# One transpose for two heads' last keys, zero-padded V tails, PV dots in every iteration: a change to a fused attention and two-MoE kernel

## Chip, cores, metric

One core of a Trainium2 chip runs the whole program: TensorE (matmuls and transposes), VectorE, ScalarE, GpSimd (named POOL in the profile), SyncE (named SP, which issues the copies), and 16 DMA engines that carry them out. The metric is the device time of one execution in microseconds (us), the median of three runs.

## What is computed

```python
# q, k, v: (4 batches, 8 heads, 576 keys, 64); tau a scalar
scores = scale * np.matmul(q, k.transpose(0, 1, 3, 2))
thresh = np.max(scores, axis=-1, keepdims=True) - tau
scores = np.where(scores >= thresh, scores, -1e9)
attn = np.exp(scores - np.max(scores, axis=-1, keepdims=True))
attn = attn / (np.sum(attn, axis=-1, keepdims=True) + 1e-09)
o = np.matmul(attn, v)
# o becomes x: (2304, 512); then two layers of this form, w_in (512, 2048), w_out (2048, 512):
h = x @ w_in; g = h - tanh(h); x = g @ w_out        # second layer: g = h * sigmoid(h)
```

## The kernel before

The attention part fills the first 327 us, the two layers the rest; the change touches the attention part alone.

*Tiling.* The 32 heads form 16 pairs (NPAIR), each two heads of one batch. A head's 576 keys are four chunks of 128 (SM = 512 keys) and a last one of 64 (SL); its 576 queries likewise. A query tile is 128 queries of one head; the ninth tile of a pair holds the last 64 queries of both heads. Two tiles form a `Double`, and one iteration n starts one Double. Two pairs 2u and 2u+1 take nine Doubles (NS = 9), so n runs over 8 units of nine iterations; n below is counted within the unit. The middle Double (n = 4) has the ninth tiles of both pairs.

*Stages of a Double.* For each of its tiles x = 0, 1: `score` (TensorE, L309: f32r products of the high and low parts of q and k into PSUM; tile `s`), `peak` (VectorE, L325: row maximum, negated), `thr1` (ScalarE, L339: threshold), `exp` (ScalarE, L329); one iteration later `keep` (VectorE, L345: zero what is under the threshold, sum up), `guard` (GpSimd, L353), `inv` (VectorE, L356), `norm` (GpSimd, L360), `flip` (TensorE, L365: four transposes of e into PSUM tile `t`); `evac` copies them to `pt` (ScalarE, L380), `flip_last` transposes the last 64 keys (L375: two transposes, which place head 0's keys in rows 0 to 63 and head 1's in rows 64 to 127) and `levac` copies them to `pj` (L392). flip0 stands at the end of the iteration after the score, flip1 and flip_last in the one after that.

*PV.* `Out` is one half (288 queries) of a pair's output: for each of five key chunks one f32 matmul ("dot") for each head, head 0 into rows 0 to 63 of PSUM tile `a`, head 1 into rows 64 to 127. The device runs every f32 dot as two passes. The last chunk's dots take 64 rows each of `pj` and of `vn` (L411, form 64*64 in the profile). `AVS` gives how many dots an iteration runs: 6 and 4 in turn, from n = 6 on, none at n = 5. `store` copies `a` to `ao` (L419) and, with the second half, to xT by DMA (L424 to L427), and then loads V of the pair after next.

*Preparing a pair.* `PREP` gives the iteration, relative to its unit, of each step for the even and the odd pair: t (four transposes of the loaded K or Q, tile `nat`, L229), f (copy back), left (transposes of the last keys and queries, L234), h (high parts, VectorE L261, with the DMA moves kh and qp, L249), l (low parts, GpSimd L274, with the moves of kl and qp; it then issues the load of the next pair's K or Q, L216). `nat` has one buffer for K and one for Q.

*Order.* The first layer's weights are decoded along the way (`DECS`: six stages of three chains, L118 to L148). `ORDER` is the order in which an iteration issues its actions. TensorE, VectorE, ScalarE and GpSimd execute their instructions in that order; the copies on SyncE's queue are placed by a planner, by when they can run, and execute one after the other, each waiting for its own conditions with all later ones behind it.

## Time and profile before

| | |
|---|---|
| median of three runs | 1106.5 us (1105.49 to 1106.54) |
| the profiled execution | 1106.72 us |
| its span, first to last instruction | 1104.9 us |
| TensorE, share of the span busy | 98% |
| VectorE, ScalarE, GpSimd busy | 72%, 71%, 34% |
| attention part | to 327 us; a unit of nine iterations takes 38.1 us |
| DMA engines busy in the attention part | about 77% |

The times of the rows below are us from the start of the span. A timeline row has its start, its length (from the first start to the last end of equal instructions that follow each other), engine, line, operation, tile written <- tiles read, shape, count, and in brackets the idle time of the engine before it and what ended that. A matmul's recorded length (0.27 to 0.45 us) is longer than the step to the next one, since matmuls are pipelined; steps are therefore read from start to start.

### The profile page before, as it was taken

Reading aid. Unit: us, or ns where it says so; the run is one execution under the profiler, and the core shown is the slowest. Engines: PE = TensorE matmul, PEld = TensorE weight load, DVE = VectorE, ACT = ScalarE, POOL = GpSimd, SP = SyncE. Lnnn points to the kernel's source line nnn. Section 1 sums busy time; section 2 is a strip of 40 time slices with the busy share of each in tenths; the row PEclk is TensorE's granted clock in tenths of the full one; section 3 lists DMA queues with packets and bytes.
Section 4 is the critical chain, followed back from the end, with each engine's and each line's share of the span. In section 5 each row is a group of like instructions: output and inputs, shape, how many; then the busy total and the mean of one; then the engine's idle time right before and its main releaser. Section 6 shows DMA issues by size and latency. Waiting matters only on the chain.

```text
span 1104.9 us, 17846 instructions
## 1 busy us (share of the span) xinstructions
PE 1086.0 (98%) x6028; PEld 903.2 (82%) x6028; DVE 799.1 (72%) x1492; ACT 780.6 (71%) x1628; POOL 370.7 (34%) x414
## 2 busy tenths in 40 slices
PE   8999999999999999999999999999999999999998
PEld 6677767777768888888889988888989899889986
DVE  5888888888857876666665678877768665775553
ACT  5999989999879887777777888855545443454342
POOL 4666766776632435334432233322100000000000
PEclk8999999999999999999999999999999999999999
DMA  8578777877633313223321011244323221232111
GB/s 207 129 189 222 194 185 196 220 194 187 167 114 149 96 43 139 107 94 133 116 76 39 1 39 58 67 148 155 122 58 95 82 65 50 63 115 68 50 32 57
DMA packets 104298, 124.93 MB, mean 113 GB/s; under 512 B 47760, under 2 KB 71824, under 8 KB 103184
## 3 DMA queue, kind: packets, MB, share of 16 engines
q1 hardware_dynamic: 104208, 123.80, 39.0%
q8 instruction: 48, 0.79, 0.3%
q14 instruction: 42, 0.34, 0.1%
HBM read 73.93 MB, written 17.30 MB: 83 GB/s over the span
## 4 chain that ended last, share of the span: by engine, by line
PE 94%; DVE 2%; DMA 1%; issue 1%; ACT 1%; SPq 0%; POOL 0%; DVEq 0%; POOLq 0%; ACTq 0%
PE bank L943 18%; PE bank L626 18%; PE bank L679 17%; PE bank L1038 16%; PE s L309 8%; PE a L411 8%; PE t L365 6%; PE t L375 2%; PE t L229 1%; DVE e L345 1%; DVE kh L261 1%; DMA nat<-in_k_dram 0%; SPq L216 0%; POOL e L360 0%; PE t L234 0%
## 5 line engine op out<-in xcount | busy, mean ns | idle before, releaser
L679 PE MATMUL bank<-g_r,wo 128*128 128x512 f32 (+1 forms) x960 | 211.0, 368 | 0.2 <-DVE g_r L665 0.2
L626 PE MATMUL bank<-xs_r,wr 128*128 128x512 f32 (+1 forms) x640 | 193.3, 368 | 0.0
L679 PEld LDWEIGHTS bank<-g_r,wo 128*128 128x128 f32 x960 | 168.4, 189 | 30.0 <-DVE g_r L665 0.4
L1038 PE MATMUL bank<-wr 128*128 128x384 f32 x816 | 189.2, 337 | 1.4 <-DVE tm_r L980 1.4
L645 POOL TENSOR_TENSOR tm_r<-tm_r 128x512 f32<-128x512 f32 (+1 forms) x78 | 96.6, 1238 | 233.1 <-ACT tm_r L640 227.6
L1038 PEld LDWEIGHTS bank<-wr 128*128 128x128 f32 x816 | 146.5, 188 | 7.1 <-DVE tm_r L980 2.2
L360 POOL TENSOR_SCALAR e<-e,den 128x576 f32<-128x576 f32 x144 | 113.8, 802 | 61.1 <-DVE den L356 51.2
L626 PEld LDWEIGHTS bank<-xs_r,wr 128*128 128x128 f32 x640 | 117.2, 189 | 20.5 <-issue 0.4
L325 DVE TENSOR_REDUCE c<-s 128x1 f32<-128x576 f32 x144 | 108.3, 753 | 33.3 <-PE s L309 30.5
L345 DVE SCALAR_TENSOR_TENSOR e<-s,c,e 128x576 f32<-128x576 f32 x144 | 115.4, 813 | 13.5 <-ACT e L329 13.5
L626 PE MATMUL bank<-xT,wr 128*128 128x512 f32 (+1 forms) x320 | 117.8, 368 | 0.0
L980 DVE TENSOR_TENSOR tm_r<-bank,tm_r 128x384 f32<-128x384 f32 x120 | 66.5, 554 | 67.9 <-PE bank L1038 66.6
L1000 ACT ACTIVATE tm_r<-tm_r 128x384 f32<-128x384 f32 x72 | 37.8, 525 | 107.0 <-DVE tm_r L980 106.7
L943 PE MATMUL bank<-wo,g_r 128*128 128x512 f32 x432 | 109.8, 392 | 0.0
L943 PE MATMUL bank<-wo,xs_r 128*128 128x512 f32 x432 | 108.8, 392 | 0.0
L329 ACT ACTIVATE e<-s,c 128x576 f32<-128x576 f32 x144 | 105.4, 732 | 0.2
L647 DVE TENSOR_TENSOR tm_r<-bank,tm_r 128x512 f32<-128x512 f32 (+1 forms) x80 | 51.0, 637 | 68.7 <-ACT tm_r L646 68.5
L943 PEld LDWEIGHTS bank<-wo,g_r 128*128 128x128 f32 x432 | 80.5, 188 | 14.7
L943 PEld LDWEIGHTS bank<-wo,xs_r 128*128 128x128 f32 x432 | 80.5, 188 | 14.4
L365 PE MATMUL t<-ident,e 128*128 128x128 f32 x576 | 83.3, 281 | 4.0 <-POOL e L360 3.1
L365 PEld LDWEIGHTS t<-ident,e 128*128 128x128 f32 x576 | 62.0, 141 | 30.7 <-POOL e L360 22.9
L657 DVE COPY_PREDICATED tm_r<-tm_r 128x512 f32<-128x512 uint32 (+1 forms) x80 | 69.6, 870 | 6.8
(126 smaller groups left out, 2008.0 us busy)
## 6 DMA issues: line engine op xcount, KB each, us to landing
wr<-pair SPq DMA_DIRECT2D x72, 256.0 KB, 3.2
st_r<-in_moe_w_out_dram SPq DMA_DIRECT2D x24, 512.0 KB, 3.6
kh<-kh SPq DMA_DIRECT2D x60, 144.0 KB, 2.6
raw<-in_moe_w_in_dram SPq DMA_DIRECT2D x16, 512.0 KB, 5.6
st_r<-in_moe_w_in_dram SPq DMA_DIRECT2D x16, 512.0 KB, 3.6
pair<-st_r SPq DMA_DIRECT2D x8, 1024.0 KB, 3.9
qp<-qh SPq DMA_DIRECT2D x30, 160.0 KB, 3.7
qp<-ql SPq DMA_DIRECT2D x30, 160.0 KB, 3.3
```

Of the source, the lines that this page charges most:

```text
L309: nc.tensor.matmul(out=s[:, j, 0:HALF], lhsT=l, rhs=r(slice(j * HALF, (j + 1) * HALF)), start=(x == 0), stop=(x == len(mms) - 1))
L325: nc.vector.tensor_reduce(out=self.c[:, x:x + 1], in_=self.s[x], axis=AX.XY, op=ALU.max, negate=True)
L329: nc.scalar.activation(out=e.rearrange("p (a b) -> p a b", a=2), in_=self.s[x], func=ACTF.Exp, bias=self.c[:, x:x + 1], scale=1.0)
L345: nc.vector.scalar_tensor_tensor(out=e2, in0=self.s[x], scalar=self.c[:, 2 + x:3 + x], in1=e2, op0=ALU.is_ge, op1=ALU.mult, accum_out=self ...
L360: nc.gpsimd.tensor_scalar(out=e, in0=e, scalar1=self.den[:, 2 + x:3 + x], scalar2=1.0, op0=ALU.mult, op1=ALU.mult)
L365: nc.tensor.transpose(t[:, c, :], self.e[x][:, c * P:(c + 1) * P], ident)
L411: nc.tensor.matmul(out=self.a[r], lhsT=lhs, rhs=rhs, start=(c == 0), stop=(c == NC))
L626: nc.tensor.matmul(out=h, lhsT=wi[:, a, cs], rhs=b, start=(c == 0 and x == 0), stop=(c == KD - 1 and x == 2))
L645: (nc.vector if u[0] == 0 and u[1] in PM else nc.gpsimd).tensor_tensor(out=r, in0=r, in1=uu, op=ALU.mult)
L679: nc.tensor.matmul(out=o, lhsT=wo[:, a, cs], rhs=b, start=(m == 0 and x == 0), stop=(m == KF - 1 and x == 2))
L943: nc.tensor.matmul(out=o, lhsT=l[:, cs], rhs=r, start=(g == 0 and low and x == 0), stop=(g == NG - 1 and not low and x == 2))
L1038: nc.tensor.matmul(out=acc, lhsT=w[:, at(a, c):at(a, c) + P], rhs=b[:, c], start=(k not in (2, 5, 6) and c == 0 and x == 0), stop=(c == 1 ...
```

## The change

- K of head 1 is loaded in another order of keys: the last 64 keys first, then the 512 others. For pairs 1 to 15 a K load has five copies for two. `e` of both tiles is one buffer of 2 x 576 columns, so head 0's last 64 keys and head 1's last 64 keys lie side by side, and one transpose of 128 columns takes the place of two. The flips of head 1 start at column 64. In the ninth tile (n = 4), whose rows belong to both heads, head 1's score products are written back into the common order, with three matmuls (288, 224 and 64 columns) for two.
- V's last keys lie in `vz`, one tile for each parity of pair, 128 rows per head, of which the other head's 64 rows are zero. The last chunk's dots have 128 rows. Two copies for one.
- `AVS` gives 5, 5, 6, 4, 5, 5, 4, 5 and 1 dots in iterations 6, 7, 8, 0, 1, 2, 3, 4, 5.
- One threshold instruction for both tiles (`thr`), after exp 0.
- Each half output is stored by its own DMA (`AOH`); V's load is an action of its own (`v`), an iteration after the store.
- `PREP`: the odd pair's K transposes and copy back one iteration earlier. `DECS` and `ORDER` anew.

```diff
-PREP = ({'tk': -6, 'fk': -5, 'left': -4, 'hk': -4, 'lk': -4, 'tq': -4, 'fq': -3, 'hq': -3, 'lq': -3},
-        {'tk': -1, 'fk': 0, 'left': 0, 'hk': 0, 'lk': 0, 'tq': 0, 'fq': 1, 'hq': 1, 'lq': 1})
-DECS = ((-4, -3, -2, -1, -1, -1), (0, 1, 2, 3, 3, 4), (2, 3, 4, 4, 6, 7))
-AVS = (6, 4, 6, 4, 6, 4, 6, 4)
-AVX = (0, 0, 0, 0, 0, 0, 0, 0)
-
-ORDER = (0, 10, 'flip1', 'f', 'evac0', 'store', 'evac1', 'keep0', 'score0', 'last', 'levac', 'keep1', 'guard', 3, 12, 'dx', 'score1', 'peak0', 'thr0', 'exp0', 'inv', 'norm0', 'norm1', 2, 13, 'peak1', 'thr1', 'exp1', 1, 11, 'dy', 't', 'warm', 'flip0', 4, 14, 'h', 5, 15, 'moves', 'l')
+PREP = ({'tk': -6, 'fk': -5, 'left': -4, 'hk': -4, 'lk': -4, 'tq': -4, 'fq': -3, 'hq': -3, 'lq': -3}, {'tk': -2, 'fk': -1, 'left': 0, 'hk': 0, 'lk': 0, 'tq': 0, 'fq': 1, 'hq': 1, 'lq': 1})
+DECS = ((-4, -2, -2, -1, -1, 0), (0, 2, 3, 4, 4, 4), (-1, 3, 3, 4, 7, 7))
+AOH = 1
+AVS = (((6, 5), (7, 5)), ((8, 6), (9, 4)), ((10, 5), (11, 5)), ((12, 4), (13, 5), (14, 1)))
+
+ORDER = (2, 'f', 'flip1', 'v', 11, 'keep0', 'score0', 'keep1', 3, 'store', 'evac0', 'evac1', 5, 1, 'guard', 'last', 10, 'peak0', 'inv', 0, 'norm0', 'levac', 13, 14, 'score1', 'norm1', 'peak1', 12, 4, 'dots', 'warm', 'exp0', 'h', 'thr', 'exp1', 'moves', 15, 'l', 't', 'flip0')
...
+                src = a[b, h0:h0 + 2, 0:SM, :].rearrange("h (p c) d -> p c h d", c=NC)
+                last = a[b, h0:h0 + 2, SM:S, :].rearrange("h p d -> p h d")
+                if x or p == 0:
+                    parts = [(t[:, 0:NC].rearrange("p c h d -> p (c h) d"), src), (t[0:SL, NC, :, :], last)]
+                else:
+                    parts = [(t[:, 0:NC, 0, :], src[:, :, 0]), (t[SL:P, 0:NC, 1, :], src[0:SL, :, 1]),
+                             (t[0:SL, 1:NC + 1, 1, :], src[SL:P, :, 1]), (t[0:SL, NC, 0, :], last[:, 0]), (t[0:SL, 0, 1, :], last[:, 1])]
                 return [lambda o=o, i=i: nc.sync.dma_start(out=o, in_=i) for o, i in parts]
...
+                vn = vns[p] = vn_p.tile([P, 2 * NC, D], F32, tag="vn", name="vn")
                 nc.sync.dma_start(out=vn[:, 0:2 * NC, :].rearrange("p (h c) d -> p h (c d)", h=2),
                                   in_=v[b, h0:h0 + 2, 0:SM, :].rearrange("h (p c) d -> p h (c d)", c=NC))
-                nc.sync.dma_start(out=vn[:, 2 * NC, :], in_=v[b, h0:h0 + 2, SM:S, :])
+                for h in range(2):
+                    nc.sync.dma_start(out=vz[p % 2][h * SL:(h + 1) * SL, h, :], in_=v[b, h0 + h, SM:S, :])
...
+                    mms = [(qh[:, cs], kl[x], x) for x in heads] + [(qp[:, x, cs], kp[:, x], x) for x in heads]
+                for i, (l, r, x) in enumerate(mms):
                     for j in range(2):
-                        nc.tensor.matmul(out=s[:, j, 0:HALF], lhsT=l, rhs=r(slice(j * HALF, (j + 1) * HALF)),
-                                         start=(x == 0), stop=(x == len(mms) - 1))
+                        if x == 0 or t < NS - 1:
+                            cuts = [(0, HALF, j * HALF)]
+                        else:
+                            cuts = ([(0, HALF, SL)], [(0, SM - HALF, SL + HALF), (SM - HALF, HALF, 0)])[j]
+                        for y, z, f in cuts:
+                            nc.tensor.matmul(out=s[:, j, y:z], lhsT=l, rhs=r[:, f:f + z - y], start=(i == 0),
+                                             stop=(i == len(mms) - 1), skip_group_check=len(heads) > 1)
...
+                        both = sm_p.tile([P, 8], F32, tag="c", name="c")
+                        self.c, self.den = both[:, 0:4], both[:, 4:8]
...
-                    e = self.e[x] = e_p.tile([P, S], F32, tag="e", name="e")
+                    if x == 0:
+                        self.both = e_p.tile([P, 2 * S], F32, tag="e", name="e")
+                    e = self.e[x] = self.both[:, x * S:(x + 1) * S]
...
+                def thr(self):
+                    nc.scalar.activation(out=self.c[:, 2:4], in_=self.c[:, 0:2], func=ACTF.Identity, bias=neg_tau, scale=-1.0)
...
+                    at = SL if x and self.tiles[x][0] and self.tiles[x][1] < NS - 1 else 0
                     for c in range(NC):
-                        nc.tensor.transpose(t[:, c, :], self.e[x][:, c * P:(c + 1) * P], ident)
+                        nc.tensor.transpose(t[:, c, :], self.e[x][:, at + c * P:at + (c + 1) * P], ident)
...
                 def flip_last(self):
-
                     t = self.tj = ps_t.tile([P, 4 * P], F32, tag="t", name="t")
...
+                    if self.tiles[0][1] == NS - 1:
+                        cuts = [(x, x, h) for x in range(2) for h in (1, 0)]
+                    elif self.tiles[0][0] == 0:
+                        cuts = [(0, h, h) for h in (1, 0)]
+                    else:
+                        nc.tensor.transpose(t[:, 0:P], self.both[:, SM:SM + P], ident)
+                        return
+                    for at, x, h in cuts:
+                        nc.tensor.transpose(t[0:(h + 1) * SL, at * P:(at + 1) * P], self.e[x][:, SM - h * SL:S], ident)
...
-                        lhs, rhs = (vn[:, h * NC + c, :], pt[:, h, c, js]) if c < NC else (vn[r, 2 * NC, :], pj[r, js])
+                        lhs, rhs = (vn[:, h * NC + c, :], pt[:, h, c, js]) if c < NC else (vz[self.p % 2][:, h, :], pj[:, js])
...
+                    if AOH:
+                        b, hp = divmod(self.p, HP)
+                        ao = ao_p.tile([P, HALF], F32, tag=f"ao{self.j}", name="ao")
+                        nc.scalar.copy(out=ao, in_=self.a)
+                        dst, at = xF[:, hp, b * S:(b + 1) * S], self.j * HALF
+                        cuts = [(at, at + HALF)]
+                        if b % 2 and self.j:
+                            cuts = [(at, SM), (SM, S)]
+                        for x, y in cuts:
+                            to = x if b % 2 == 0 else (x + SL if x < SM else x - SM)
+                            nc.sync.dma_start(out=dst[:, to:to + y - x], in_=ao[:, x - at:y - at])
+                        return
...
+            for z in vz:
+                for h in range(2):
+                    nc.gpsimd.memset(z[(1 - h) * SL:(2 - h) * SL, h, :], 0.0)
...
-            for go in (k1l, q1l, k1, q1):
+            for go in (*lk1[3:], q1l, *lk1[0:3], q1):
...
                             if o.j == 1 and o.p + 2 < NPAIR:
-                                load_v(o.p + 2)
+                                vloads.append(o.p + 2)
+
+                    def vload():
+                        while vloads:
+                            load_v(vloads.pop(0))
```

## Rows read from the trace of the kernel before

**Rows 1.** Page, part 4: the chain of waits, shares by engine
```profile
PE 94%; DVE 2%; DMA 1%; issue 1%; ACT 1%; SPq 0%; POOL 0%; DVEq 0%; POOLq 0%; ACTq 0%
```

**Rows 2.** Windows, five periods of 38.1 us: busy us by engine, mean last
```profile
sum 190.50, PE 187.33 PEld 136.64 DVE 163.29 ACT 175.04 POOL 132.71; mean PE 37.47 PEld 27.33 DVE 32.66 ACT 35.01 POOL 26.54
```

**Rows 3.** Timeline of TensorE's matmuls: start us, length, work, [idle before]
```profile
228.16 0.60 PE L229 MATMUL t<-ident,nat 128*128 128x128 f32 x4
228.94 1.38 PE L365 MATMUL t<-ident,e 128*128 128x128 f32 x8 [0.19 <-POOL e L360]
230.70 0.53 PE L309 MATMUL s<-kl,qh 128*128 128x288 f32 x2 [0.39 <-DVE e L345]
...
234.00 1.09 PE L365 MATMUL t<-ident,e 128*128 128x128 f32 x8
234.92 0.50 PE L309 MATMUL s<-kl,qh 128*128 128x288 f32 x2
...
235.53 0.38 PE L375 MATMUL t<-ident,e 128*128 128x128 f32 x2
235.74 0.51 PE L309 MATMUL s<-xT,qh 128*128 128x288 f32 x2
...
236.44 0.71 PE L411 MATMUL a<-pt,vn 128*64 128x288 f32 x4
...
237.71 1.22 PE L365 MATMUL t<-ident,e 128*128 128x128 f32 x8
...
240.34 1.68 PE L411 MATMUL a<-pt,vn 128*64 128x288 f32 x12
241.95 0.66 PE L229 MATMUL t<-ident,nat 128*128 128x128 f32 x4
242.44 1.04 PE L365 MATMUL t<-ident,e 128*128 128x128 f32 x8
```

**Rows 4.** Timeline of SyncE's queue, the even pair's moves and K load
```profile
229.94 2.44 SPq L249 DMA_DIRECT2D kh<-kh  x4
232.79 0.47 SPq L249 DMA_DIRECT2D xT<-kl  x1
233.38 1.46 SPq L216 DMA_DIRECT2D nat<-in_k_dram  x2
234.93 1.20 SPq L249 DMA_DIRECT2D qp<-qh  x2
```

**Rows 5.** Timeline of TensorE, the last output's dots
```profile
323.96 2.16 PE L411 MATMUL s<-pt,vn 128*64 128x288 f32 x16
326.06 0.70 PE L411 MATMUL s<-pj,vn 64*64 64x288 f32 x4
```

**Rows 6.** Lines of ScalarE, 55 to 284 us: threshold; busy us, mean ns
```profile
L339 ACT ACTIVATE c<-c,cols 128x1 f32<-128x1 f32 x108 | 32.1, 297 | 13.5 <-DVE c L325 11.7
```

**Rows 7.** Timeline of VectorE: kh's cast in n=5; peak 1 and keep 0
```profile
229.03 0.89 DVE L261 CAST kh<-nat 128x576 fp32r<-128x576 f32 x1
...
240.76 0.73 DVE L325 TENSOR_REDUCE c<-s 128x1 f32<-128x576 f32 x1
241.76 0.82 DVE L345 SCALAR_TENSOR_TENSOR e<-s,c,e 128x576 f32<-128x576 f32 x1 [0.27 <-ACT e L329]
```

**Rows 8.** DMA issues, 55 to 284 us: count, KB, median us to landing
```profile
nat<-in_k_dram SPq DMA_DIRECT2D x12, 32.0 KB, 3.3
```

**Rows 9.** Tile nat, 55 to 284 us: K and Q loads, issue to landing
```profile
DMA to landing us min/median/max: 2.8/3.6/5.0
```

**Rows 10.** Timeline of SyncE's queue: the odd pair's last qp moves
```profile
217.81 1.18 SPq L249 DMA_DIRECT2D qp<-ql  x2
```

**Rows 11.** Timeline of TensorE: that pair's first use of qp
```profile
223.59 0.69 PE L309 MATMUL s<-kh,qp 128*128 128x288 f32 x4
```

**Rows 12.** Timeline of TensorE at the start: pair 1's K transposes
```profile
10.88 1.07 PE L229 MATMUL t<-ident,nat 128*128 128x128 f32 x4 [2.43 <-DMA nat<-in_k_dram]
```

**Rows 13.** Waits of weight loads, 55 to 284 us: total, times, longest
```profile
PEld t L365 <- POOL e L360: 14.0, 39, 0.4
```

More of the change, by code (lines that the diff above doesn't have):

```diff
@@ L180 @@
             pk_p = pool("pk", 1)
-            e_p = pool("e", 4)
+            e_p = pool("e", 2)
             sm_p = pool("sm", 6)
@@ L195 @@
             khs = [pk_p.tile([P, 2, S], F32R, name=f"kh{i}") for i in range(2)]
+            vz = [pk_p.tile([P, 2, D], F32, name=f"vz{i}") for i in range(2)]
             nat, vns, qhs, pts = {}, {}, {}, {}
@@ L339, in thr1 @@
                         nc.scalar.activation(out=o, in_=i, func=ACTF.Identity, bias=neg_tau, scale=-1.0)
+                def thr(self):
+                    nc.scalar.activation(out=self.c[:, 2:4], in_=self.c[:, 0:2], func=ACTF.Identity, bias=neg_tau, scale=-1.0)
                 def keep(self, x):
-                    if x == 0:
-                        self.den = sm_p.tile([P, 4], F32, tag="den", name="den")
                     e2 = self.e[x].rearrange("p (a b) -> p a b", a=2)
@@ L363, in flip @@
                     t = self.tt[x] = ps_t.tile([P, NC, P], F32, tag="t", name="t")
+                    at = SL if x and self.tiles[x][0] and self.tiles[x][1] < NS - 1 else 0
                     for c in range(NC):
-                        nc.tensor.transpose(t[:, c, :], self.e[x][:, c * P:(c + 1) * P], ident)
+                        nc.tensor.transpose(t[:, c, :], self.e[x][:, at + c * P:at + (c + 1) * P], ident)
                 def flip_last(self):
                     t = self.tj = ps_t.tile([P, 4 * P], F32, tag="t", name="t")
-                    self.copies = []
-                    for x, (p, ti) in enumerate(self.tiles):
-                        for h in ((1, 0) if ti == NS - 1 else () if x == 0 else (1, 0)):
-                            js = x if ti == NS - 1 else 0
-                            e = self.e[x if ti == NS - 1 else h]
-                            nc.tensor.transpose(t[0:(h + 1) * SL, js * P:(js + 1) * P], e[:, SM - h * SL:S], ident)
+                    if self.tiles[0][1] == NS - 1:
[7 more added lines that the diff above has]
+                        nc.tensor.transpose(t[0:(h + 1) * SL, at * P:(at + 1) * P], self.e[x][:, SM - h * SL:S], ident)
                 def evac(self, x):
@@ L427, in store @@
                             nc.sync.dma_start(out=dst, in_=ao)
-            avs = {6 + i: (i // 4, i // 2 % 2, AVX[i], n - AVX[i]) for i, n in enumerate(AVS)}
+            assert all(sum(n for _, n in split) == 2 * NC + 2 for split in AVS)
+            avs = {i: (o // 2, o % 2, n) for o, split in enumerate(AVS) for i, n in split}
             outs, aos = {}, {}
             def av_at(n):
-                for i, (x, j, nx, ny) in avs.items():
+                for i, (x, j, k) in avs.items():
                     u, r = divmod(n - i, NS)
                     if r == 0 and 0 <= u < NPAIR // 2:
-                        return outs.setdefault((2 * u + x, j), Out(2 * u + x, j)), nx, ny
-                return None, 0, 0
+                        return outs.setdefault((2 * u + x, j), Out(2 * u + x, j)), k
+                return None, 0
             def due(table, n):
@@ L474 @@
             his, ts, dbl, later = {}, {}, {}, []
-            (k0, k0l), (q0, q0l), (k1, k1l), (q1, q1l) = load(0, 0), load(0, 1), load(1, 0), load(1, 1)
+            (k0, k0l), (q0, q0l), lk1, (q1, q1l) = load(0, 0), load(0, 1), load(1, 0), load(1, 1)
             for go in (k0, q0, k0l, q0l):
@@ L558, in moves @@
                             later.pop(0)()
-                    acts = {"last": last_keys, "levac": last_evac, "store": store, "moves": moves,
-                            "dx": lambda: dots(nx), "dy": lambda: dots(ny),
+                    acts = {"last": last_keys, "levac": last_evac, "store": store, "moves": moves, "v": vload,
+                            "dots": lambda: dots(dots_n),
                             "t": lambda: some("t", transposed), "f": lambda: some("f", filled),
@@ L573 @@
                     acts["inv"] = lambda: d1 and d1.inverse()
+                    acts["thr"] = lambda: d0 and d0.thr()
                     for what in ORDER:
```

15 lines of the change are left out of this document (4 added, 11 removed).

## Prediction

> **What bounds the kernel now.** I read the chain of waits first: TensorE holds 94% of it [rows 1]. Then the attention part by stretches of 38.1 us, since everything repeats with one "period" of nine iterations n = 0 to 8 (two pairs of heads; there are eight periods). In a period TensorE is busy for 37.47 us, ScalarE for 35.01, VectorE for 32.66, GpSimd for 26.54 [rows 2]: TensorE sets the pace, ScalarE is close behind. Then TensorE's timeline [rows 3]. It is nearly gapless; the one real hole is the iteration without PV dots, n = 5. There the flips start 0.78 us after the four K/Q transposes (228.16 to 228.94), where the same step takes 0.49 later (241.95 to 242.44), and the eight flips last 1.76 us until the scores (228.94 to 230.70) where 0.92 is enough (234.00 to 234.92): 1.1 us of waiting for GpSimd's norm and VectorE's keep. So what TensorE has to do counts almost one to one, and what engines beside it save counts little. Last I read SyncE's queue, which issues every copy, one after the other; from the kh moves on it has hardly a pause [rows 4].
>
> **The change part by part.** The terms are made against the profiled execution: 1106.72 us, of which 1104.9 are the span; the median of the runs is 1106.5, 0.2 below it.
>
> *On TensorE.* (a) One transpose for both heads' last keys: two take 0.21 us (235.53 to 235.74), one goes, in 60 iterations (15 pairs by 4): -6.3. (b) A slot of dots (one pass of each head): 12 passes take 1.61 us (240.34 to 241.95) [rows 3] and 16 take 2.10 (323.96 to 326.06) [rows 5]. Two slots cost 0.49, one 0.24. The four slots of a session that ends in the 64-row form last 1.27 (236.44 to 237.71); without a change of form they would last 1.61 - 0.49 = 1.12. The zero-padded V saves 0.15 for each of 32 outputs: -4.8. (c) Nine sessions of dots in a period, not eight; beside its slots a session has a fixed part of 1.61 - 6 x 0.24 = 0.17: +1.4 over eight periods. (d) The new sessions have 5, 5, 6, 4, 5, 5, 4, 5 and 1 dots. Dots alternate between the heads, and an odd number leaves one head's two passes alone in the array: 5 dots take 6 slots, 1 takes 2. That is 46 slots a period against 40: 6 x 0.24 x 8 = +11.5. No session of before is odd. If a lone head's two passes could share a slot the price would be 0; I take 11.5, because no two passes in the rows take less than 0.24. (e) The last query tile needs three score matmuls for two in head 1's rotated order, 30 more of 64 columns: 0 at the least, if they hide beside their weight loads, 0.105 at the most, a transpose's price as in (a). Taken 0.1: +3.0. Sum: +4.8. But the lone dot falls into n = 5, where TensorE waits for 1.1 us, and its 2 x 0.24 + 0.17 = 0.65 hides there: -5.2. If that hole closes in another way, the 5.2 are due. Net: -0.4.
>
> One rule speaks about (d). The Trainium skill, "TensorE: Matmul & The Clock Gate", section "The mechanism" on packing small matmuls, says that matmuls start and end strictly in program order. With both passes of head 0 ahead of both of head 1, 6 dots would then take 7 slots, 4 take 5 and 5 take 6; a period would go from 48 slots to 49, and (d) would be 1.9. The trace speaks against it: seven slots and nine slots of 0.24 are 1.68 and 2.16 us, and the rows have 1.61 and 2.10 with the fixed part in them [rows 3, 5].
>
> *ScalarE and the new wait.* One threshold instruction for two takes 0.3 us an iteration [rows 6] off an engine that does not end last: 0. In exchange head 0's keep waits for head 1's peak as well. Behind that keep stand keep 1 and both peaks on VectorE, and TensorE's next scores wait for it. Peak 1 starts at 240.76 and takes 0.73; with 0.3 for the threshold keep 0 could start at 241.8, and it starts at 241.76 now [rows 7]: 0 to 0.1 an iteration, 7 in all at most, and less than nothing where the threshold now comes late on ScalarE. Taken 0, since TensorE's work per iteration is mostly longer than this loop.
>
> *SyncE's queue: the K load.* This term decides. Head 1's keys are rotated at loading, by five copies where there were two, for 15 pairs. And PREP moves the odd pair's K transposes from n = 8 to n = 7, while their load is still issued in n = 5, behind the even pair's kl. Follow one period. VectorE casts kh from 229.03 to 229.92 [rows 7]; SyncE issues four kh moves from 229.94, the kl move at 232.79 and K's load from 233.38; two issues last until the next at 234.93, so 0.73 or more each [rows 4]. Of five the last is issued at 233.38 + 4 x 0.73 = 236.3. A small K copy lands 3.3 us after its issue in the median [rows 8], all K and Q copies between 2.8 and 5.0 [rows 9]: 239.6 (239.1 to 241.3). In n = 7 the transposes stand between dots and flips, at 237.71 now; six slots for four of the old form add 0.34, the transpose saved in n = 7 takes 0.11 off: 237.9. TensorE works in order, so flips and the next scores queue behind. It stands for 1.7 us (1.2 to 3.4) in each of seven periods: +11.9. Before, these transposes came at 241.95 [rows 3], over two us after 239.6: that was the cover, and the move takes it away. The Q load behind it in the queue comes 2.2 us later too, but the stall itself gives that time back.
>
> *qp of the odd pair.* Its last move is issued at 218.4 [rows 10]; 3.3 later is 221.7, 5.0 later 223.4, and the scores want it at 223.59 [rows 11]. Three more K issues (2.2) stand ahead of it, V's two copies leave. So it is late by 0 to 1 us a period: taken 0.3 x 7 = +2.1.
>
> *Start.* TensorE waits 2.43 us for pair 1's K [rows 12]; now two more issues of 0.73 stand ahead of its last large piece: +1.5. *At nothing:* half outputs stored one by one (16 issues more, 0.7 each at most on SyncE, after the moves in n = 6), V's load as an action of its own, four small memsets beside the first loads, decode steps that change places on engines with 3 to 11 us free in a period [rows 2]; if one lands ahead of a peak or an exp it costs up to an iteration's share of that work, which the range holds.
>
> Sum: -0.4 + 11.9 + 2.1 + 1.5 = +15.1, so 1121.8, and 1122 as a median.
>
> **The rivals.** *1. The copies are in time, and waits go.* If K's pieces are issued ahead of the moves or land sooner, 11.9 and 2.1 fall away. With dots in every iteration and less on ScalarE, waits for GpSimd's norm may go as well: 14.0 us in six periods [rows 13], 2.3 a period, of which up to 1.1 is spent above. Half of the rest is 0.6 x 8 = 5: 1106.7 - 0.4 + 1.5 - 5 = 1103, 1098 if all goes. For it: the planner places copies by when they are ready. Against: all five wait for the buffer that the kl subtraction reads, and the kh moves are ready before. Chance 0.23. *2. The copies are in time and nothing else is won:* 1106.7 - 0.4 + 1.5 = 1108; 0.12. *3. SyncE falls behind altogether:* with three K, one V and up to two output issues more between the even pair's kh moves and the odd one's, the odd pair's moves slip by their 6 x 0.73 less the pauses, 1 to 2 us beyond the forecast, in each period: 1122 + 7 x 1.5 = 1132; 0.12. For it: qp's slack is under two us. Against: the stall in n = 7 gives SyncE time. *4. Matmuls in program order,* as weighed in (d): 1122 - 9.6 = 1112; 0.03.
>
> **How the numbers follow.** The forecast, 1122, has 0.50. Its bounds: 1.2 to 3.4 for the K stall (1118 to 1134), 0 for lone dots (1110), 7 for the new wait (1129). The range, 1100 to 1132, leaves out the half of rival 3 and about a third of rival 1, under 2 in 10 with the forecast's own upper edge. About 0.2% can be told from no change. Faster: rival 1 and 0.01 of rival 2, 0.24; same: 0.09 of rival 2; slower: the forecast, rivals 3 and 4 and 0.02 of rival 2, 0.67.
>
> **What the profile after would show.** K stall: once a period TensorE's K transposes wait for the load from in_k, one to three us, behind the dots. (a), (b): one transpose between the two scores, no 64-row dots. (d): 5 dots last as long as 6, 1.6 us. n = 5 without its 1.1 us. The prediction is wrong if the K load lands before the dots of n = 7 end; then the time is near 1105, and nearer 1095 if lone passes cost nothing.

## The result, and the profile after

The changed kernel takes 1114.5 us in the median (1111.4 to 1116.2), the kernel before 1106.5 on the same chip: a ratio of 1.0067, 95% interval 1.0049 to 1.0086. It is slower by 8.0 us, where 15.5 were forecast. The profiled execution has a span of 1113.8 us, 8.9 more than before.

Where the 8.9 lie, read from TensorE's timeline: the first score starts at 11.76 (11.88 before). The seven periods from there last 274.8 (269.5 before): +5.3. From the last period's start to the first matmul of the layers it is 46.6 (45.3): +1.3. The layers take 780.54 (778.25): +2.3. But the periods are no longer equal. They last 42.7, 38.9, 37.8, 40.3, 38.4, 38.8 and 38.0; before, all but the first two were 38.1. TensorE's waits, 15 to 325 us (in total, times, longest), name the reason:

```profile
PE t L234 <- DMA nat<-in_k_dram: 4.0, 3, 1.7
PE t L380 <- POOL e L374: 2.8, 7, 0.9
PE t L239 <- DMA nat<-in_q_dram: 2.6, 3, 1.3
PE s L319 <- DVE e L359: 1.6, 4, 0.5
PE t L234 <- ACT e L342: 1.2, 1, 1.2
```

L234 are the K transposes, L239 those of the last keys and queries. The line with "ACT e" is a load as well: at 166.34 the transposes start 0.09 after K's last piece has landed, when that exp had long ended. Two periods on TensorE's timeline, n = 7 and what follows (columns as in [rows 3]):

```profile
85.26 0.94 PE L428 MATMUL a<-pt,vn 128*64 128x288 f32 x5
85.80 0.41 PE L428 MATMUL a<-pj,vz 128*64 128x288 f32 x1
86.04 0.41 PE L428 MATMUL a<-pt,vn 128*64 128x288 f32 x1
86.04 0.88 PE L428 MATMUL a<-pj,vz 128*64 128x288 f32 x3
88.26 0.63 PE L234 MATMUL t<-ident,nat 128*128 128x128 f32 x4 [1.33 <-DMA nat<-in_k_dram]
...
237.89 1.67 PE L428 MATMUL a<-pt,vn 128*64 128x288 f32 x10
239.49 1.09 PE L380 MATMUL t<-ident,e 128*128 128x128 f32 x8
...
241.72 0.94 PE L428 MATMUL a<-pt,vn 128*64 128x288 f32 x5
...
243.32 0.66 PE L234 MATMUL t<-ident,nat 128*128 128x128 f32 x4
...
245.94 1.68 PE L428 MATMUL a<-pt,vn 128*64 128x288 f32 x12
247.54 1.32 PE L380 MATMUL t<-ident,e 128*128 128x128 f32 x8
```

In the first period TensorE waits 1.33 for K, and its transposes start at 88.26; in the other they follow the dots without a pause, at 243.32, 0.33 after K's last piece landed. The same rows show the slots: 10 passes last 1.60 (237.89 to 239.49), 12 last 1.60 (245.94 to 247.54). Now SyncE's queue in the same two periods, with [rows 4] to compare:

```profile
78.66 3.97 SPq L254 DMA_DIRECT2D kh<-kh  x4
82.73 0.54 SPq L254 DMA_DIRECT2D xT<-kl  x1
83.37 3.30 SPq L220 DMA_DIRECT2D nat<-in_k_dram  x5
...
235.17 2.41 SPq L254 DMA_DIRECT2D kh<-kh  x4
237.68 0.55 SPq L254 DMA_DIRECT2D xT<-kl  x1
238.32 3.25 SPq L220 DMA_DIRECT2D nat<-in_k_dram  x5
```

Five issues take 3.25 to 3.30, 0.66 each. What differs is ahead of them: four kh moves take 2.41 in one period and 3.97 in the other, since the fourth, at 80.53, lasts 2.10 where 0.6 is usual. The fifth piece was issued at 86.08 and landed at 88.12. By size of the copy, 55 to 284 us (count, KB, median us to landing; the answer to [rows 8]):

```profile
nat<-in_k_dram SPq DMA_DIRECT2D x12, 128.0 KB, 2.7
nat<-in_k_dram SPq DMA_DIRECT2D x24, 64.0 KB, 2.8
nat<-in_k_dram SPq DMA_DIRECT2D x24, 16.0 KB, 2.3
```

The two small pieces land 2.3 us after their issue in the median, the last of them mostly 2.0 to 2.3, not 3.3. TensorE stands for K in four of the seven periods. In three of these a kh move ahead of the load lasts 1.5 to 2.1 us; in the fourth the last piece lands 3.5 us after its issue (162.71 to 166.25). In the other three periods it lands 0.25 to 0.36 us ahead of TensorE.

### The profile page after: what moved, and what is told of

Read it like the earlier page. It is cut to its first block, busy times and chain, and to the rows that moved or that the text cites. A ratio compares the mean times of both kernels' runs of the same rounds, so it can differ in the third digit from the quotient of the medians.

```text
span 1113.8 us, 17983 instructions
## 1 busy us (share of the span) xinstructions
PE 1087.3 (98%) x5998; PEld 908.6 (82%) x5998; DVE 802.2 (72%) x1492; ACT 772.5 (69%) x1556; POOL 372.7 (33%) x418
## 3 DMA queue, kind: packets, MB, share of 16 engines
q1 hardware_dynamic: 107712, 123.80, 38.4%
## 5 line engine op out<-in xcount | busy, mean ns | idle before, releaser
L374 POOL TENSOR_SCALAR e<-e,c 128x576 f32<-128x576 f32 x144 | 116.4, 821 | 71.8 <-DVE c L370 61.7
L359 DVE SCALAR_TENSOR_TENSOR e<-s,c,e 128x576 f32<-128x576 f32 x144 | 111.5, 810 | 12.9 <-ACT c L355 12.9
L1038 ACT ACTIVATE tm_r<-tm_r 128x384 f32<-128x384 f32 x72 | 37.8, 525 | 106.1 <-DVE tm_r L1018 106.0
L428 PE MATMUL a<-pt,vn 128*64 128x288 f32 x496 | 80.7, 419 | 0.0
```

Of the source, the lines that this page charges most:

```text
L359: nc.vector.scalar_tensor_tensor(out=e2, in0=self.s[x], scalar=self.c[:, 2 + x:3 + x], in1=e2, op0=ALU.is_ge, op1=ALU.mult, accum_out=self ...
L374: nc.gpsimd.tensor_scalar(out=e, in0=e, scalar1=self.den[:, 2 + x:3 + x], scalar2=1.0, op0=ALU.mult, op1=ALU.mult)
L428: nc.tensor.matmul(out=self.a[r], lhsT=lhs, rhs=rhs, start=(c == 0), stop=(c == NC))
```

## The experiments

All were timed beside the kernel before on the same chip. The last column is the difference of the two medians; the median of the kernel before moves by 1.2 us between the chips.

| kernel | median us | ratio to before, 95% interval | us to before |
|---|---|---|---|
| changed kernel | 1114.5 | 1.0067 (1.0049 to 1.0086) | +8.0 |
| changed, K by two copies, unrotated | 1105.4 | 0.9989 (0.9979 to 0.9999) | -1.2 |
| changed, K transposes moved back | 1112.2 | 1.0055 (1.0033 to 1.0077) | +5.7 |
| changed, even dots | 1110.7 | 1.0036 (1.0024 to 1.0048) | +4.2 |
| changed, halves stored together | 1115.3 | 1.0080 (1.0068 to 1.0093) | +8.7 |
| changed, K rotated on ScalarE | 1110.5 | 1.0043 (1.0030 to 1.0057) | +4.1 |
| the same, even dots ("R") | 1105.5 | 0.9998 (0.9988 to 1.0007) | -0.9 |
| R, two thresholds | 1109.1 | 1.0035 (1.0022 to 1.0047) | +3.7 |
| R, last transpose twice | 1109.1 | 1.0030 (1.0019 to 1.0042) | +3.8 |
| R, one buffer for half outputs | 1106.4 | 1.0005 (0.9996 to 1.0014) | +1.0 |
| before, five copies of K | 1112.0 | 1.0057 (1.0041 to 1.0074) | +5.6 |
| before, K transposes earlier | 1103.8 | 0.9987 (0.9977 to 0.9996) | -1.6 |
| before, both | 1108.9 | 1.0027 (1.0017 to 1.0038) | +2.9 |
| before, 5 dots everywhere | 1115.1 | 1.0080 (1.0065 to 1.0094) | +8.7 |
| before, one threshold | 1106.6 | 1.0009 (1.0001 to 1.0018) | +0.6 |
| before, padded V | 1144.1 | 1.0344 (1.0330 to 1.0358) | +38.1 |
| before, padded V, one threshold, K earlier | 1137.6 | 1.0294 (1.0272 to 1.0316) | +31.6 |
| before, padded V loaded later | 1105.1 | 0.9991 (0.9982 to 1.0000) | -0.5 |
| the same, K earlier | 1104.3 | 0.9987 (0.9978 to 0.9996) | -1.3 |

The length of an iteration (from one score 0 to the next on TensorE's timeline), in a period without a wait for a load, is what most of the readings below rest on (median over such periods):

| n | 0 | 1 | 2 | 3 | 4 | 5 | 6 | 7 | 8 | sum |
|---|---|---|---|---|---|---|---|---|---|---|
| before | 4.47 | 3.96 | 3.77 | 4.42 | 4.63 | 4.37 | 4.22 | 3.90 | 4.40 | 38.1 |
| changed, K by two copies | 4.20 | 3.97 | 3.91 | 3.90 | 5.11 | 4.03 | 4.23 | 4.31 | 3.84 | 37.5 |
| changed, K rotated on ScalarE | 4.20 | 3.97 | 3.91 | 3.90 | 5.12 | 4.04 | 4.33 | 4.32 | 4.56 | 38.4 |
| R | 4.20 | 3.98 | 3.91 | 3.90 | 4.86 | 4.03 | 4.33 | 3.89 | 4.50 | 37.6 |
| R, two thresholds | 4.19 | 3.98 | 3.91 | 3.91 | 4.68 | 4.04 | 4.68 | 3.91 | 4.77 | 38.1 |
| R, last transpose twice | 4.36 | 4.00 | 3.91 | 3.91 | 4.97 | 4.37 | 4.15 | 4.09 | 4.49 | 38.2 |
| before, 5 dots everywhere | 4.93 | 3.96 | 4.05 | 4.33 | 5.09 | 4.37 | 4.22 | 4.10 | 4.33 | 39.4 |
| before, K transposes earlier | 4.46 | 3.96 | 3.76 | 4.42 | 4.63 | 4.37 | 4.22 | 4.06 | 3.95 | 37.8 |
| before, padded V loaded later | 4.32 | 3.96 | 3.77 | 4.42 | 4.56 | 4.37 | 4.22 | 3.90 | 4.40 | 37.9 |

### The copies of K

Two copies in the changed kernel, which leave out the rotation of head 1's keys, so that its keys and values do not fit together:

```diff
-                if x or p == 0:
+                if True:
                     parts = [(t[:, 0:NC].rearrange("p c h d -> p (c h) d"), src), (t[0:SL, NC, :, :], last)]
...
```

> The changed kernel with K loaded by two copies as before, in the common order of keys; head 1's rotation is left out of the load, while everything behind it works as if it were there, so head 1's keys and values do not fit together and that part of the computation is changed. The instructions on all other engines are the same. Theory (three more issues on SyncE's queue in each period make K late at n = 7 and Q's last queries late at n = 0): both stalls go, 5 and 3.5 us in the trace of the changed kernel, and with the start some 9 us: 1105.5. Rival (the stalls come from moving the K transposes, not from the number of copies; SyncE's queue is late with two as well): 0 to 3 us, 1111 to 1114.

Measured: -1.2 to the kernel before, 9.1 less than the changed kernel. Every period but the first lasts 37.5, and no wait for K or Q is left. So the five copies cost 9.1 us, and all the rest of the change together gains about 1. That 1 is what is left of two opposite parts: in the profiled executions the first matmul of the layers starts 3.4 us earlier than in the kernel before (323.28 for 326.69), and the layers take 2.95 longer (781.20 for 778.25). Of this trace, TensorE's waits to 315 us:

```profile
PE t L380 <- POOL e L374: 2.5, 6, 0.8
PE s L319 <- DVE e L359: 1.1, 3, 0.4
```

The K transposes moved back in the changed kernel (the odd pair's part of `PREP`):

```diff
-... {'tk': -2, 'fk': -1, 'left': 0, ...
+... {'tk': -1, 'fk': 0, 'left': 0, ...
```

> The changed kernel with the odd pair's K transposes and copy back where they were before (n = 8 and n = 0 for n = 7 and n = 8), all else as changed. Theory (the K load with five copies lands after the dots of n = 7): in the trace of the changed kernel n = 7 lasts 5.37, 5.68, 4.32, 5.57, 5.25, 4.21 us, an excess of about 5 us in all over 4.2; with the transposes an iteration later, the load has landed, so about 5 us less: 1109.5, and n = 7 of one length of some 3.8 us in all periods. Rival (the queue of copies is behind in any case and the stall moves to the next step that waits for a load, Q's last keys at n = 0): no gain, 1113 to 1116, and n = 0 or n = 8 longer by what n = 7 loses.

Measured: 2.2 less, not 5, and the two intervals overlap. The stall at n = 7 went (4.0 to 4.1 in all periods), but n = 0 now lasts 5.1, 5.7, 4.6, 5.5, 7.6, 4.6, 4.2, where 4.2 is its length with two copies. The last columns wait for Q, the load behind K in the queue (in the longest of these, the scores ahead of them also stand 0.8 us for the kl and qp moves); TensorE's timeline of this kernel:

```profile
166.04 0.28 PE L239 MATMUL t<-ident,nat 64*128 64x64 f32 x1
167.33 0.27 PE L239 MATMUL t<-ident,nat 64*128 64x64 f32 x1 [1.02 <-DMA nat<-in_q_dram]
```

That is the rival. The changed kernel shows the same by itself: its n = 7 lasts 6.1, 5.7, 4.3, 5.6, 5.2, 4.3, 4.4 (the expectation's 5.37 for the first counts from its score 1) and the n = 0 behind each 4.2, 4.4, 5.7, 4.2, 5.2, 4.2, 4.9. Where K has stalled, Q mostly does not, and the other way round: the queue's lateness is paid about once a period, by the first step that needs a load.

In the kernel before, K by five copies in the old order of keys, the move, and both:

```diff
-                parts = [(main, a[b, h0:h0 + 2, 0:SM, :].rearrange("h (p c) d -> p c h d", c=NC)),
-                         (t[0:SL, NC, :, :], a[b, h0:h0 + 2, SM:S, :].rearrange("h p d -> p h d"))]
...
+                    parts = [(t[:, 0:NC, 0, :], src[:, :, 0]), (t[0:SL, 0:NC, 1, :], src[0:SL, :, 1]),
+                             (t[SL:P, 0:NC, 1, :], src[SL:P, :, 1]), (t[0:SL, NC, 0, :], last[:, 0]), (t[0:SL, NC, 1, :], last[:, 1])]
...
-... {'tk': -1, 'fk': 0, 'left': 0, ...
+... {'tk': -2, 'fk': -1, 'left': 0, ...
```

> The kernel before, with K of pairs 1 to 15 loaded by five copies for two, in the old order of keys; all else as before, the K transposes at n = 8. Prediction's steps: K lands over two us before its transposes, so only the start (1.5) and the odd pair's qp (2.1) cost: 1110. Theory formed from the run with the transposes moved back (the queue pays for its three issues once in a period, at the first step that needs a load, and that is then Q's last columns at n = 0): n = 0 some 1 us longer in each period, 1112 to 1115. Rival (five copies cost nothing where the transposes are not moved): 1106.5.

> The kernel before with the odd pair's K transposes and copy back one iteration earlier, as in the change, and nothing else: two copies of K. In its trace K lands at 238.0 where TensorE would come to the transposes at 237.7. Theory (the number of copies is what costs, the move by itself little): 0 to 0.3 us a period, 1106.5 to 1108.5. Rival (the cover of over two us that the move takes away is the price, as the prediction has it): 1 us a period or more, 1113 and up.

> The kernel before with K in five copies and the odd pair's K transposes one iteration earlier, both together, in the old order of keys: the two edits that the prediction's main term is made of, alone. Prediction's step (the fifth piece lands 1.7 us after TensorE comes to the transposes, in each of seven periods; qp and the start on top): 1106.5 + 15.5 = 1122. Theory after the runs so far (the queue's lateness is paid once a period, less its slack, wherever the first step stands that waits): as with five copies and no move, 1110 to 1114.

Five copies in the old order of work cost 5.6, more than the 3.6 of the prediction's steps, though K lands in time: in four of seven periods n = 4, where qp of the odd pair is first used, is up to 1.1 longer, and n = 0 or n = 3 in others. In one of the four TensorE stands 0.57 us ahead of scores that read qp (108.72), in another 0.44 ahead of those that read kl (186.08). The move alone gains 1.6 (n = 8 falls from 4.40 to 3.95, n = 7 grows from 3.90 to 4.06). Both together cost 2.9, which is 4.4 more than the move alone, and not 15.5. There n = 7 has no stall, 4.05 to 4.17 in all seven periods; what is late is again n = 3, n = 4 or n = 0. So with these two edits alone the stall that the prediction names does not occur.

The rotation without more copies, on ScalarE where the transposes are copied back:

```diff
+                if x == 0 and p:
+                    nc.scalar.copy(out=flat(p, 0)[0:D, 0:SM], in_=t[0:D])
+                    nc.scalar.copy(out=flat(p, 0)[D:P, SL:S], in_=t[D:P])
+                    return
...
```

> The changed kernel with K loaded by two copies in the common order; head 1's keys are brought into the rotated order where ScalarE copies the transposes back (two copies of half the partitions for one, at two places, for each K: about 0.9 us more on ScalarE, twice in a period). Theory (five copies on SyncE's queue are what costs): as with the unrotated load of two copies, 1105.4, plus 0 to 3 us for ScalarE where its copy holds an exp up: 1105 to 1109, and n = 7 and n = 0 of one length in all periods. Rival (ScalarE sets the iteration's length as much as TensorE, so 1.8 us a period come back in full): 1105.4 + 14 = 1119.

Measured: 3.8 less than the changed kernel, between theory and rival. The periods are equal again, 38.4, but n = 8 lasts 4.56 for 3.84 with two copies alone. Its timeline there, of ScalarE, VectorE and TensorE:

```profile
199.98 0.58 ACT L246 COPY nat<-t 64x512 f32<-64x512 f32 x1 [0.38 <-ACT e L350]
200.57 0.59 ACT L247 COPY nat<-t 64x512 f32<-64x512 f32 x1
...
204.16 0.82 DVE L367 SCALAR_TENSOR_TENSOR e<-s,c,e 128x576 f32<-128x576 f32 x1 [1.30 <-ACT c L363]
205.09 0.50 PE L327 MATMUL s<-kl,qh 128*128 128x288 f32 x2 [0.39 <-PE t L388]
```

ScalarE copies K back in two pieces of 0.6 us for one, its exps and threshold come later, VectorE's keep 0 waits 1.30 for the threshold (0.52 with two copies alone), and the next score 0 starts behind keep 0, which ends at 204.98.

### The dots

```diff
-AVS = (((6, 5), (7, 5)), ((8, 6), (9, 4)), ((10, 5), (11, 5)), ((12, 4), (13, 5), (14, 1)))
+AVS = (((6, 6), (7, 4)), ((8, 6), (9, 4)), ((10, 6), (11, 4)), ((12, 4), (13, 4), (14, 2)))
```

> The changed kernel with even numbers of dots in every iteration: 6, 4, 6, 4, 6, 4, 4, 4, 2 for 5, 5, 6, 4, 5, 5, 4, 5, 1. Theory (a dot without its partner of the other head costs a slot of its own of 0.24 us): six slots fewer in each of eight periods, 6 x 0.24 x 8 = 11.5 us less: 1103. Rival 1 (program order, any number of dots costs one slot more than half its number): 49 slots either way, no change, 1114.5. Rival 2 (slots saved in some iterations are not TensorE's to give, since VectorE and ScalarE set the length there): half or less of it, 1108 to 1112.

> The same kernel, K by two copies and rotated on ScalarE, with even numbers of dots (6, 4, 6, 4, 6, 4, 4, 4, 2). With no stall for a load in the way, this is the price of a dot without its partner by itself. Theory of the prediction (0.24 us for each of 48 slots): 11.5 us less than the kernel with odd numbers. Rival (an iteration cannot be shorter than the loop from a score over peak, reciprocal, two norms and a flip to the next score, 3.9 us, and most iterations of the changed kernel are at or near it): the 0.24 us at n = 4 alone comes back, 1 to 3 us less.

In the kernel before:

```diff
-AVS = (6, 4, 6, 4, 6, 4, 6, 4)
+AVS = (5, 5, 5, 5, 5, 5, 5, 5)
```

> The kernel before with 5 dots in each of eight iterations, for 6 and 4 in turn. Prediction's price (a dot without its partner takes a slot of 0.24 us, and TensorE is the bound): four iterations of a period get two slots more, 8 x 0.24 x 8 = 15.4: 1122. Rival 1 (two of these four iterations, n = 2 and n = 7 of 3.76 and 3.89 us, are set by the loop over VectorE and GpSimd and hide most of it; n = 0 and n = 4 pay): 7 to 10 us, 1114 to 1117. Rival 2 (program order, 5 and 5 cost as many slots as 6 and 4): 1106.5.

Measured: 3.8 less with the loads in the way, 5.0 less without (kernel R against the same with odd dots), 8.7 more for 5 dots everywhere in the kernel before. That is a third to little more than half of 0.24 a slot (11.5, 11.5, 15.4), and the table of iterations tells where the rest is lost. In the kernel before, two slots more cost 0.46 at n = 0 and n = 4, 0.28 at n = 2 and 0.20 at n = 7. In kernel R two slots less give back 0.43 at n = 7 and 0.26 at n = 4, and nothing at n = 2: 3.91 either way. Its timeline there, of TensorE, VectorE and GpSimd:

```profile
211.56 0.51 PE L327 MATMUL s<-kl,qh 128*128 128x288 f32 x2
212.38 0.76 DVE L344 TENSOR_REDUCE c<-s 128x1 f32<-128x576 f32 x1 [0.43 <-PE s L327]
213.05 0.15 DVE L378 RECIPROCAL c<-c 128x2 f32<-128x2 f32 x1
213.37 1.63 POOL L382 TENSOR_SCALAR e<-e,c 128x576 f32<-128x576 f32 x2 [0.47 <-DVE c L378]
...
214.17 0.66 PE L388 MATMUL t<-ident,e 128*128 128x128 f32 x4
215.06 0.66 PE L388 MATMUL t<-ident,e 128*128 128x128 f32 x4 [0.23 <-POOL e L382]
215.47 0.51 PE L327 MATMUL s<-kl,qh 128*128 128x288 f32 x2
```

Score 0 at 211.56, its peak at 212.38, behind it on VectorE the reciprocal at 213.05, the two norms from 213.37 to 215.00, flip 1 at 215.06, the next score 0 at 215.47: 3.91 round. TensorE waits 0.23 for the norm. With five dots it does not wait, and the iteration lasts as long. This loop closes in every iteration and is a floor under it; TensorE's work counts only where it is longer.

### The other parts

The transpose that the change saves, issued twice in R, and two thresholds in R:

```diff
+                        nc.tensor.transpose(t[:, P:2 * P], self.both[:, SM:SM + P], ident)
                         nc.tensor.transpose(t[:, 0:P], self.both[:, SM:SM + P], ident)
...
-... 'exp0', 'h', 'thr', 'exp1', ...
+... 'thr0', 'exp0', 'h', 'thr1', 'exp1', ...
```

> The same kernel of 1105.5 with the one transpose of both heads' last keys issued twice, the first into a part of the tile that nobody reads: the price of the transpose that the change saves. Prediction's step (TensorE counts almost one to one, 0.105 x 60): 6.3 us more, 1111.8. Rival (the iterations that lie on the loop over peak, reciprocal, norms and flip hide it, n = 1, 2, 3 above all): 1 to 3 us, 1106.5 to 1108.5.

> The kernel with K by two copies, rotated on ScalarE, and even dots (1105.5), with two threshold instructions as before, each ahead of its exp or behind it as it was, so that head 0's keep no longer waits for head 1's peak; ScalarE has some 0.3 us more in each iteration. Prediction's step (the merged threshold and its wait are worth nothing either way): 1105.5. Rival 1 (the new wait holds keep 0 up by up to 0.1 us in each of 72 iterations): 3 to 7 us less, 1099 to 1102. Rival 2 (ScalarE's 0.2 to 0.3 us an iteration are due where its exps stand on the loop): 3 to 10 us more, 1109 to 1115.

One more transpose in 60 iterations costs 4.7 (3.8 + 0.9); the prediction had 6.3. It is not 0.1 in each: n = 0, 4, 5 and 7 grow by 0.16, 0.11, 0.34 and 0.20, n = 6 shrinks by 0.18, and n = 1, 2, 3 and 8 stay as they were within 0.02. Two thresholds cost 4.6, where the prediction had 0; the table shows it at n = 6 (+0.35) and n = 8 (+0.27), with n = 4 shorter by 0.18. In the kernel before the merged threshold gains nothing:

```diff
-... 'peak0', 'thr0', 'exp0', 'inv', 'norm0', 'norm1', 2, 13, 'peak1', 'thr1', 'exp1', ...
+... 'peak0', 'exp0', 'inv', 'norm0', 'norm1', 2, 13, 'peak1', 'thr', 'exp1', ...
```

> The kernel before with one threshold instruction for both tiles, behind exp 0 as in the change; nothing else. Undoing this edit in the other kernel cost 0.47 us in each period. Theory (0.3 us less on ScalarE ahead of exp 0 and exp 1 counts in the iterations that lie on the loop over exp): 3 to 4 us less, 1102.5 to 1103.5. Prediction's step (nothing either way): 1106.5. Rival (head 0's keep waits for head 1's peak and threshold): up to 7 us more, 1108 to 1113.

There n = 2 grows from 3.77 to 3.96 and n = 4 from 4.63 to 4.76, which n = 3, n = 6 and n = 8 nearly give back: +0.6. So the merged threshold's worth depends on the order around it; which waits make n = 6 and n = 8 of R longer with two was not traced further.

Zero-padded V in the kernel before, its load right behind the output's store, and then one iteration later as in the change (the last two):

```diff
-                nc.sync.dma_start(out=vn[:, 2 * NC, :], in_=v[b, h0:h0 + 2, SM:S, :])
+                for h in range(2):
+                    nc.sync.dma_start(out=vz[p % 2][h * SL:(h + 1) * SL, h, :], in_=v[b, h0 + h, SM:S, :])
...
-... (vn[r, 2 * NC, :], pj[r, js])
+... (vz[self.p % 2][:, h, :], pj[:, js])
...
-                                load_v(o.p + 2)
+                                vloads.append(o.p + 2)
```

> The kernel before with V's last keys zero-padded for each head (128 rows in the last dots, no 64-row form), loaded by two copies for one; nothing else. Prediction's step: 0.15 for each of 32 outputs, 4.8 us less, 1101.7. Theory after the runs so far (of what TensorE saves, the iterations with n = 2 and n = 7, near the floor of 3.8 to 3.9 us, give back little): about half, 2 to 4 us less, 1102.5 to 1104.5. Rival (the 15 copies more on SyncE's queue take it back): 1106.5 or more.

> The kernel before with three parts of the change and without the rotated K: one threshold instruction, V's last keys zero-padded, the odd pair's K transposes one iteration earlier. Theory (these are the parts that gain, the five copies and the odd numbers of dots are those that cost): -1.5 for the move as measured, -3 to -4 for the threshold, -2 to -5 for V: 1096 to 1100. Rival (they all shorten the same iterations and do not add up): 1100 to 1103.

> The kernel before with V's last keys zero-padded, loaded by two copies for one, and V's load issued an iteration later than the output's store, as the change does it; nothing else. In the run without that delay SyncE came to V's load ahead of the odd pair's kh moves and waited there for V's buffer, and n = 4 lasted 10 us. Theory: with the load behind Q's, that wait is gone, and what is left is the saving in the last dots, 2 to 5 us: 1101.5 to 1104.5. Rival (one issue more for each pair on SyncE's queue costs as much as it saves): 1106.5. Second rival (the queue still comes to V too early): 1115 or more.

> The same with the odd pair's K transposes one iteration earlier (two copies of K, the old order of keys, the old dots). Theory: the move's gain of 1.5 and the saving in the last dots add up: 1100 to 1103, less than both kernels. Rival (both shorten n = 7 and n = 8, which come to the floor of 3.8 us and below which nothing is won): 1103 to 1104.5.

The first two came out 38 and 32 us slower, with n = 4 at 9 to 13 us. The expectation of the later run blames V's load ahead of the kh moves; the trace says otherwise. The load of weights for the decode (L125) had been put behind the odd pair's Q load in SyncE's queue, where in the kernel before it stood ahead of that pair's kh moves, and VectorE and ScalarE stood at the decode step until it landed, with the next peaks and copies behind it. Timeline of this kernel, SyncE, VectorE and ScalarE:

```profile
199.72 0.75 SPq L217 DMA_DIRECT2D nat<-in_q_dram  x1
200.52 0.59 SPq L125 DMA_DIRECT2D raw<-in_moe_w_out_dram  x1
...
204.66 0.43 DVE L132 TENSOR_SCALAR raw<-raw 128x512 uint32<-128x512 uint32 x1 [3.23 <-DMA raw<-in_moe_w_out_dram]
...
204.66 0.68 ACT L118 ACTIVATE raw<-raw 128x512 f32<-128x512 f32 x1 [4.08 <-DMA raw<-in_moe_w_out_dram]
```

With V's load an iteration later the old order is back, and padding is worth 0.5 us, at n = 0 (-0.15) and n = 4 (-0.07) alone; the prediction had 4.8. Together with the earlier transposes it is 1.3 below the kernel before, no more than the move alone. The move alone, and the move with padding, are the fastest kernels of the study that compute the whole, both 0.13% under the kernel before.

Two runs concern the stores and the end of the attention part, the first on the changed kernel, the second on R:

```diff
-AOH = 1
+AOH = 0
...
-... tag=f"ao{self.j}", ...
+... tag="ao0", ...
```

> The changed kernel with both halves of an output stored together again (AOH = 0). Theory: the casts of the first layer's input no longer stand behind the last half's copy on ScalarE, so TensorE's wait of 1.06 us for them at the end of the attention part goes, and the periods stay as they are: 1 us less, 1113.5. Rival 1: the 16 stores more on SyncE's queue are part of what makes the K and Q loads late; then 3 us or more less, 1111.5. Rival 2: the casts' place has another cause, no change, 1114.5.

> The same kernel of 1105.5 with one buffer for the half outputs on their way out instead of two. It changes the order on ScalarE at the end of the attention part: the first of the four casts of the first layer's input stands ahead of the last half's copy. Theory (TensorE's wait of 1.06 us for these casts is a matter of that order): the wait falls to 0.3 to 0.5, 0.7 us less, 1104.8. Rival (the layers absorb it in waits of their own): 1105.5. Second rival (with one buffer a copy waits for the store ahead of it and holds ScalarE in each period): 1108 or more.

In the changed kernel the casts of the layers' first input stand behind the last half's copy on ScalarE, and TensorE waits for them:

```profile
332.25 0.40 ACT L435 COPY ao<-s 128x288 f32<-128x288 f32 x1 [2.00 <-PE s L428]
...
333.21 0.73 PE L664 MATMUL bank<-xs_r,wr 128*128 128x512 f32 x2 [1.06 <-ACT xs_r L650]
```

Halves stored together leave the order and the time as they are. With one buffer for the halves the first cast comes ahead and the wait of 1.06 is gone from the trace, but the time is not lower. In the layers the changed kernel and those made from it lose 0.9 to 3.2 us on the kernel before; of the nine made from the kernel before, six lose 0.1 at the most and three 0.7 to 0.9. Most of it is one wait for an output store, here on VectorE in the kernel before and in the changed one:

```profile
979.33 0.69 DVE L950 COPY st_r<-bank 128x512 f32<-128x512 f32 x1 [0.75 <-DMA out_dram<-st_r]
...
988.02 0.69 DVE L988 COPY st_r<-bank 128x512 f32<-128x512 f32 x1 [2.23 <-DMA out_dram<-st_r]
```

In the layers SyncE and VectorE run the same instructions in the same order in both kernels. Why the store lands later is left open.

## Where the prediction was right, and where not

The direction and the cause were right: the K load in five copies decides, and TensorE stands at the K transposes of n = 7 behind the dots. The size was not. Its sum splits into the copies (11.9 + 2.1 + 1.5 = 15.5) and the rest (-0.4). Measured are 9.1 and -1.2.

*The K load, forecast 11.9 and 2.1: the term that was mis-sized.* The step that failed is the stall of 1.7 us in each of seven periods, from 0.73 an issue and 3.3 to the landing of the last piece. Issues are 0.66 apart, and the last piece mostly lands 2.0 to 2.3 after its issue. The 3.3 of [rows 8] was for a copy behind a large one (with two copies in the changed kernel it is 3.0 in the median of twelve), and this one follows other small ones; it was also thinly founded, since the trace of the kernel before has the landing of three of those twelve copies (2.85, 3.30 and 5.03) and of six of the 48 in [rows 9]. With these numbers the load lands at 233.38 + 4 x 0.66 + 2.1 = 238.1, not 239.6, and meets TensorE within 0.3, much as at 243.32. What is left is not a steady stall but the loss of slack. With two copies K's last piece lands 0.5 to 1.4 ahead of TensorE at n = 7 and Q's 0.1 to 1.9 ahead at n = 0. Three issues take 2.0 us. K's slack falls to 0.3, Q's is used up, and every copy that is late for another reason (a kh move of 1.5 to 2.1 us, a landing of 3.5) then shows. In the trace it is 5.4 us at n = 7, for 11.9, and 3.5 at n = 0, for nothing, over the length with two copies. That a stall gives Q's delay back was right for the periods that stall; in the others Q pays it, and that the forecast left out. By the prediction's own sign of being wrong, K landing before the dots of n = 7 end, it fails in three of the seven periods. That the old place of the transposes covers the load was not the whole of it: moved back, the price stays, at Q. qp was not late in the changed kernel (n = 4 lasts 5.1 in all periods from the second); in the kernel before with five copies n = 4 is 3.0 longer in all, for 2.1 forecast, with the stops for qp and kl named above.

*The start, forecast 1.5:* nothing. Pair 1's K transposes start at 10.74, before at 10.88 [rows 12].

*TensorE, forecast -0.4 net:* near in the sum, by luck, and wrong in its terms. Without the copies the attention part gains 3.4, and the layers, where the forecast had nothing, take 2.95 of it back. The premise that TensorE's work counts almost one to one was false. It was read from a period's mean [rows 2], and a mean hides that the iterations n = 1, 2 and 7 of the kernel before, and n = 1, 2 and 3 of the changed one, lie at or near the floor of the loop over VectorE and GpSimd (3.8 to 4.0). (a) was 4.7 for 6.3, (b) 0.5 for 4.8, (d) 5.0 for 11.5; (c) and (e) were not tested by themselves. The slots themselves are as forecast, 1.60 for 5 dots as for 6. Rival 4 falls with that: by it 5 dots would take a slot less than 6, and 5 dots for 4 a slot more (0.24), where n = 0 and n = 4 of the kernel before grow by 0.46. Two dots share both of their slots: at n = 7 of the changed kernel the first pass that reads pj starts at 85.80, before the last pass of the dot ahead of it, at 86.04. The rival starts from the rule that matmuls start and end strictly in program order (the Trainium skill, "TensorE: Matmul & The Clock Gate", section "The mechanism"). These rows do not speak against that rule for whole dots; the rival's mistake was to apply it to their passes. The lone dot hides at n = 5 as said (4.37 to 4.03).

*The threshold at nothing:* 4.6 in the changed order, 0.6 the other way in the old one. Whether keep 0's wait for head 1's peak costs anything was not tested by itself; where keep 0 waited 1.30 for the threshold, in the kernel rotated on ScalarE, it was ScalarE that was late.

*The rivals.* Rival 1's condition came half true: the pieces land sooner, and in three of seven periods ahead of TensorE, but that did not clear the queue behind them. With two copies, where every load is in time, the kernel takes 1105.4, between rival 1 (1103) and rival 2 (1108). Rival 3, SyncE falling behind altogether, is half true: it is late for Q too, but the stall lets it catch up.

Open remain the store that lands later in the layers, what the new `ORDER` and `DECS` are worth by themselves, and why SyncE's issues last 1.2 to 2.2 us at irregular places; between 40 and 305 us ten of them do in the changed kernel, seven in the kernel before.

## What to carry to other kernels

Before a copy is split, work out the slack of every load behind it in its queue, not of the first one alone: the lateness is paid once, at the first step that has no slack left, and moving that step moves the stall. A bound that holds for the mean of a period need not hold in its iterations: find the loop that closes from one iteration to the next, and price an edit only where its engine's work is longer than that loop. An added copy can reorder a queue that a planner fills; look for whose load now stands behind it.

## What was not expected of the hardware

A small copy lands sooner behind small ones than behind a large one. In the changed kernel V's last keys come in two copies of 16 KB: the first, behind a copy of 256 KB, lands 3.5 us after its issue in the median, the second, behind the first, 2.3. K's two pieces of 16 KB, behind others of 64 KB, take 2.3 as well. SyncE's issues, 0.5 to 0.75 us as a rule, take 1.2 to 2.2 now and then, and the landings behind them shift alike. Two heads' passes share a slot, and a head left alone pays a full one: 10 and 12 passes both last 1.60 us.
